# Value windows of chunked attention read back in fourteen strided transfers, with two tiles of their own and the query and key loads in between

## The chip, the core and the metric

The kernel runs on one core of one Trainium2 chip. The metric is device microseconds of that core for one execution, inputs and output in DRAM. The core has a matrix engine (PE; PEld is its weight load), a vector engine (DVE), an activation engine (ACT), GpSimd (POOL) and SyncE (SP). POOL, ACT and SP each issue DMA transfers on a queue of their own: in the profile q0 is POOL's (software_dynamic), q1 is SP's and q10 ACT's (hardware_dynamic). All three are served by the core's 16 DMA engines.

## The reference: what is computed

Chunked attention with memory rows, and behind it a layer of 8 experts of which each token uses two.

```
# attention: B=4, H=8, S=768, D=64; chunks of 32 queries
for c in range(24):
    keys, values of rows 32c-16 .. 32c+40 (cut at the ends), ahead of them 8 memory rows
    out[chunk c] = softmax(q k^T / 8) v
# x = attention output as [3072 tokens, 512]
logits = x @ w_gate + log1p(exp(x @ w_noise)) * noise     # 8 experts
top two experts of each token, softmax of their two logits as weights
out[token] = sum over the two of weight * relu(x @ w1[e]) @ w2[e]   # 512 -> 1024 -> 512
```

So each chunk needs a window of 56 rows of values (16 to the left, 32 of its own, 8 to the right) and 8 memory rows: 64 rows for each head.

## The kernel before

**Attention.** The four batch items (called batches here) are done one after the other, each in 3 steps of 256 tokens (`TP = 3`, `NT = 12` steps `i`, loop at L562). A step i makes the scores of step i+1 (`scores`, L402), turns the probabilities of step i (`turn_p`, L433), turns the attention rows of i-1 (`turn_x`, L466), multiplies with the values (`values`, L442), takes the exponentials of i+1 (`exps`, L428) and the router's logits of i-1 (`gate`, L475). Queries and keys of the next batch are turned by PE (`turn`, L387; `turns`, L546) in slots that `PLAN` (L558) names: for batch 1 all of it after `values` in step 1; for later batches half of the queries ahead of `values` in the middle step of the batch before, the rest and the keys behind it.

**Values.** `load_v(b)` (L119) loads a batch's values from DRAM into the tile `vn`, cast to bfloat16. `spread_v(b)` (L366) is two POOL copies that reorder them into `vp`. `window_v(b)` (L372) then writes the windows into `vb[b % 2]`, 128 partitions: partitions 0 to 63 hold the 64 rows of the even heads, 64 to 127 those of the odd heads, and in each partition lie 24 chunks of 4 heads x 64 values (24 pieces of 512 bytes). It is made of:

- one SP transfer that copies `vp` to a scratch tensor `vd[b % 2]` in DRAM (L374), 768 KB;
- two POOL transfers of the 8 memory rows, the same for all chunks (L378), 96 KB each;
- four POOL transfers from `vd` (L383): for even and for odd heads the first 32 rows of the windows (384 KB) and the other 24 (288 KB). Row r of chunk c is row r + 32c of `vd`, so a partition's 24 pieces are 32 KB apart in DRAM.

The spans (the transfers from `vd`) wait for the copy's landing. `values` (L453) reads all of `vb[b % 2]` with PE, first in step 3b.

**Order of the queues.** POOL's instructions are pinned in program order (`pin`, L70); PE, ACT, DVE and SP run in the order written too (L516). POOL's order for a batch is: memory rows and spans of batch b+1, queries and keys of batch b+2 (`load_kq`, L122), spread of batch b+2, values of batch b+3 (L567 to L573), all at the first step of batch b. Before the loop (L527 to L535) stand the spread and the window of batch 0, then load of values 1, queries and keys 1, spread 1, load of values 2. Since POOL works in order, a span that waits for the copy holds up all that is written behind it.

**Where the data lie.** One tile `w_all` (L64) holds the weights of all 8 experts, 16 KB in each partition for an expert (8 KB of w1, 8 KB of w2). While attention runs, its upper part is scratch (L102 to L111): the attention rows `xrow`, `vn`, the two `vb`, and `nat`, the loaded queries and keys of two batches. Experts 0, 1 and 2 are loaded during the last two batches (L574, L578); expert 2 lies under `nat` of batch 3.

**Behind attention.** The router finds, for each pair of experts, the list of tokens (`Route`, L233; lists and `decode`, L488). Attention rows are stored to `xd` in DRAM (`keep_x`, L484), and `gather_x` (L669) fetches the rows of one pair's list with an indirect POOL transfer. The gathers of the first 14 pairs are issued with the loads of experts 3 and 4 in between (L765 to L769). Then `mm1` (L705) and `mm2` (L723) do the two products of each expert for the pairs that use it, in the order of `blocks` (L746); the loads of experts 5 to 7 and more gathers are issued between them (`feed`, L857). `load_pair` (L839) fetches two experts' weights again for one list that ran over.

Of the kernel before, what the change touches and what calls it, by code (L numbers as in the profile page):

```python
# [12 lines left out]
BF16 = mybir.dt.bfloat16  # L13
# [9 lines left out]
def kernel(  # L23
# [40 lines left out]
    w_all = wpool.tile([128, E, WE], BF16, name="w_all")  # L64
    wflat = w_all.rearrange("p e c -> p (e c)")
    w1v = w_all[:, :, 0:KP * F].rearrange("p e (k f) -> p e k f", k=KP)
    w2v = w_all[:, :, KP * F:WE].rearrange("p e (f d) -> p e f d", f=FB)
# [9 lines left out]
    def load_expert(e):  # L77
        pin(nc.gpsimd.dma_start(out=w1v[:, e], in_=moe_w1[e].rearrange("(kp p) f -> p kp f", p=128)))
        pin(nc.gpsimd.dma_start(out=w2v[:, e], in_=moe_w2[e].rearrange("(fb p) d -> p fb d", p=128)))


    def load_part(e, i):
        h = slice(i % 2 * KP // 2, (i % 2 + 1) * KP // 2) if i < 2 else slice(i % 2 * FB // 2, (i % 2 + 1) * FB // 2)
        if i < 2:
            pin(nc.gpsimd.dma_start(out=w1v[:, e, h], in_=moe_w1[e].rearrange("(kp p) f -> p kp f", p=128)[:, h]))
        else:
            pin(nc.gpsimd.dma_start(out=w2v[:, e, h], in_=moe_w2[e].rearrange("(fb p) d -> p fb d", p=128)[:, h]))
# [14 lines left out]
    scol = [E * WE]  # L102
# [6 lines left out]
    vb = [scratch(2 * NCH * HP * D).rearrange("p (a c w) -> p a c w", a=2, c=NCH) for _ in range(2)][::-1]  # L109
# [261 lines left out]

    def window_v(b):  # L372
        t, o = vb[b % 2], vd[b % 2]
        nc.sync.dma_start(out=o[LC:LC + S, :].rearrange("(p s) c -> p (s c)", s=SO), in_=vp)  # L374
        for par in range(2):
            p0 = par * 64
            cols = slice(par * 256, (par + 1) * 256)
            pin(nc.gpsimd.dma_start(out=t[p0:p0 + NM, par], in_=mvn[b * NM:(b + 1) * NM, cols].unsqueeze(1).to_broadcast([NM, NCH, 256])))  # L378
        for par in range(2):
            p0 = par * 64  # L380
            cols = slice(par * 256, (par + 1) * 256)
            for r0, n in ((0, CH), (CH, WIN - CH)):
                pin(nc.gpsimd.dma_start(out=t[p0 + NM + r0:p0 + NM + r0 + n, par],  # L383
                                        in_=o[r0:r0 + S, cols].rearrange("(c k) w -> k c w", k=CH)[0:n]))
# [131 lines left out]
    with tc.manual_schedule(engines={ET.PE, ET.Activation, ET.DVE, ET.SP}):  # L516
# [10 lines left out]
        spread_v(0)  # L527
        window_v(0)
# [3 lines left out]
        load_v(1)  # L532
        load_kq(1)
        spread_v(1)
# [27 lines left out]
        for i in range(NT):  # L562
# [4 lines left out]
            if tp == 0 and more:  # L567
                window_v(b + 1)
                if b + 2 < B:
                    load_kq(b + 2)  # L570
                    spread_v(b + 2)
# [414 lines left out]
```

## Time and profile before

| | us |
|---|---|
| three runs, median (lowest, highest) | 363.06 (361.42, 363.59) |
| the profiled execution | 358.42 |
| its span (first to last instruction) | 356.7 |

| engine | busy us | share of span |
|---|---|---|
| PE | 285.9 | 80% |
| DVE | 170.3 | 48% |
| ACT | 136.9 | 38% |
| POOL | 134.3 | 38% |

| queue | packets | MB | share of 16 engines' time |
|---|---|---|---|
| q0 (POOL) | 34240 | 46.82 | 73.2% |
| q1 (SP) | 13920 | 6.62 | 10.9% |
| q10 (ACT) | 1668 | 3.02 | 2.4% |

The page cuts the span into 40 slices and gives the busy share of each in tenths. A group line gives line, engine, operation, out<-in, count, then busy time and mean ns of one, then the engine's idle time ahead of them and what ended most of it. A line of the waits reads: engine and tile waited <- for what: us in total, times, longest. A line of the timeline gives start, length, engine, line, operation, count, and in brackets the idle time ahead and what ended it. Transfers are listed with their size and the median time from issue to landing. Before, `w_all` is the name under which the trace shows `vb`, `vn`, `nat` and `xrow` too, since they are cut out of it: `w_all<-vd` are the spans, `w_all<-mvn` the memory rows, `w_all<-in_q_dram` the queries.

| stretch, us | PE busy us | POOL busy us | granted PE clock | GB/s of the DMA engines |
|---|---|---|---|---|
| 35 to 60 | 16.82 | 14.94 | 0.57 | 196 |
| 60 to 90 | 21.89 | 12.00 | 0.56 | 230 |
| 90 to 120 | 20.39 | 11.65 | 0.81 | 217 |
| 120 to 140 | 8.92 | 6.69 | 0.64 | 220 |
| 150 to 170 | 19.89 | 7.75 | 1.00 | 165 |
| 200 to 250 | 49.68 | 20.48 | 1.00 | 153 |

### The profile page before, as it was taken

The page shows a single profiled execution, that of the slowest core. Times are in us where ns is not written, and L with a number is a line of the kernel's source. Part 1 is how long each engine was busy: PE and PEld are TensorE (multiplying, and loading weights), DVE is VectorE, ACT ScalarE, POOL GpSimd, SP SyncE. Part 2 cuts the span into 40 slices and gives each one's busy share as a digit, 9 for nine tenths or more (in the row PEclk, how much of TensorE's full clock was granted, in tenths as well). Part 3 has the DMA queues.
Part 4 walks back from the last instruction along what each step waited for, and adds up shares of the span by engine and source line. Part 5 has one row for each costly group of instructions (what it writes and reads, how often), then busy time and mean ns, then how long its engine had stood idle before and what let it go on. Part 6 is the DMA issues. An engine that isn't in the chain of part 4 may idle for free.

```text
span 356.7 us, 7042 instructions
## 1 busy us (share of the span) xinstructions
PE 285.9 (80%) x2934; PEld 186.3 (52%) x2955; DVE 170.3 (48%) x349; ACT 136.9 (38%) x189; POOL 134.3 (38%) x181
## 2 busy tenths in 40 slices
PE   0356577777847732999999999999999999999991
PEld 0245455666736621865544465664455775565540
DVE  7656456699689885531133302954310334223221
ACT  8813645564645610144322343213243222243310
POOL 6460573354453036706530744332580122201122
PEclk9995655565687865699999999999999999999998
DMA  8999999999999999499999999961289971100012
GB/s 122 235 171 169 245 174 208 251 198 211 247 156 208 253 249 180 106 194 143 178 196 235 209 173 252 159 119 51 87 166 189 208 184 54 53 2 2 25 47 81
DMA packets 49866, 56.97 MB, mean 160 GB/s; under 512 B 16931, under 2 KB 39523, under 8 KB 49828
## 3 DMA queue, kind: packets, MB, share of 16 engines
q0 software_dynamic: 34240, 46.82, 73.2%
q1 hardware_dynamic: 13920, 6.62, 10.9%
q10 hardware_dynamic: 1668, 3.02, 2.4%
q8 instruction: 25, 0.41, 0.5%
q14 instruction: 13, 0.11, 0.1%
HBM read 70.39 MB, written 13.96 MB: 236 GB/s over the span
## 4 chain that ended last, share of the span: by engine, by line
PE 33%; issue 20%; POOL 5%; DVE 4%; DMA 3%; POOLq 1%; ACT 0%; DVEq 0%
PE p_h L714 18%; PE p_y L726 13%; POOL out_dram L677 4%; DMA out_dram<-y,main_dst 1%; DMA xTt<-xt 1%; DMA xt<-xd,main_src 1%; POOL xt L671 1%; DVE w_all L460 1%; PE p_xt L691 0%; POOL w_all L844 0%; POOLq L981 0%; DVE mx L423 0%; DVE sc L425 0%; ACT xT L472 0%; PE ps_o L453 0%
## 5 line engine op out<-in xcount | busy, mean ns | idle before, releaser
L714 PE MATMUL p_h<-xTt,w_all 128*128 128x256 bf16 (+3 forms) x669 | 102.7, 313 | 0.7 <-DVE xTt L692 0.5
L726 PE MATMUL p_y<-w_all,h 128*128 128x512 bf16 x446 | 102.3, 379 | 0.9
L714 PEld LDWEIGHTS <-w_all 128*128 128x128 bf16 x736 | 70.0, 101 | 36.3 <-issue 0.7
L702 ACT ACTIVATE h<-p_h 128x512 bf16<-128x512 f32 (+1 forms) x81 | 44.7, 551 | 95.9 <-PE p_h L714 88.3
L726 PEld LDWEIGHTS <-h 128*128 128x128 bf16 x464 | 45.3, 98 | 51.6
L700 DVE TENSOR_SCALAR h<-p_h 128x512 bf16<-128x512 f32 (+1 forms) x49 | 31.0, 633 | 82.8 <-PE p_h L714 73.7
L677 POOL DMA_INDIRECT out_dram<-y,main_dst x28 | 30.9, 1103 | 87.9 <-DVE y L732 75.4
L732 DVE SCALAR_TENSOR_TENSOR y<-p_y,main_w,y 128x512 f32<-128x512 f32 x28 | 21.0, 750 | 39.2 <-PE p_y L726 32.5
L393 PE MATMUL p_t<-identb,w_all 128*64 128x128 bf16 x384 | 20.6, 288 | 23.0 <-DMA w_all<-in_k_dram 13.4
L671 POOL DMA_INDIRECT xt<-xd,main_src x28 | 27.9, 997 | 24.2 <-DMA xTt<-xt 13.0
L730 ACT ACTIVATE y<-p_y,main_w 128x512 f32<-128x512 f32 x28 | 19.2, 687 | 37.0 <-PE p_y L726 36.0
L393 PEld LDWEIGHTS <-w_all 128*64 128x64 bf16 x384 | 18.1, 155 | 25.2 <-DMA w_all<-in_k_dram 13.9
L439 ACT COPY pT<-p_p 128x1024 bf16<-128x1024 bf16 x12 | 12.1, 1012 | 27.5 <-PE p_p L436 27.5
L383 POOL DMA_DIRECT2D w_all<-vd x16 | 11.8, 747 | 23.8 <-DMA vd<-vp 19.3
L460 DVE TENSOR_TENSOR w_all<-ps_o,rs 128x512 bf16<-128x512 f32 x24 | 15.6, 686 | 8.2 <-PE ps_o L453 7.8
L415 PE MATMUL ps_s<-kT,qT 128*32 128x112 bf16 x384 | 11.6, 276 | 7.2 <-DVE kT L549 5.4
L368 POOL COPY vp<-w_all 128x1536 bf16<-128x1536 bf16 x8 | 11.5, 1469 | 13.2 <-DMA w_all<-in_v_dram 13.2
L430 ACT ACTIVATE pb<-sc 128x1024 bf16<-128x1024 f32 x12 | 12.8, 1063 | 8.9 <-DVE sc L425 8.7
L549 DVE COPY kT<-p_t 64x768 bf16<-64x768 bf16 x12 | 11.5, 955 | 7.9 <-PE p_t L393 7.8
L425 DVE TENSOR_TENSOR sc<-ps_s,mx 128x1024 f32<-128x1024 f32 x12 | 14.7, 1225 | 0.8
L423 DVE TENSOR_REDUCE mx<-ps_s 128x16 f32<-128x1024 f32 x12 | 14.7, 1224 | 0.8 <-PE ps_s L415 0.5
L453 PE MATMUL ps_o<-w_all,pT 128*32 128x128 bf16 x384 | 10.9, 280 | 3.3 <-issue 2.0
(172 smaller groups left out, 284.0 us busy)
## 6 DMA issues: line engine op xcount, KB each, us to landing
w_all<-in_moe_w_dram POOLq DMA_DIRECT2D x16, 1024.0 KB, 20.7
w_all<-in_moe_w_dram POOLq DMA_DIRECT2D x8, 512.0 KB, 13.8
w_all<-in_v_dram POOLq DMA_DIRECT2D x4, 768.0 KB, 12.1
w_all<-in_k_dram POOLq DMA_DIRECT2D x4, 768.0 KB, 20.9
w_all<-in_q_dram POOLq DMA_DIRECT2D x4, 768.0 KB, 18.1
vd<-vp SPq DMA_DIRECT2D x4, 768.0 KB, 9.0
w_all<-vd POOLq DMA_DIRECT2D x8, 384.0 KB, 13.0
w_all<-vd POOLq DMA_DIRECT2D x8, 288.0 KB, 13.3
```

Source lines behind the costliest of these rows:

```text
L393: nc.tensor.transpose(out=p_t[own(par), s, :], in_=src[:, 2 * pair + par, s * D:(s + 1) * D], identity=identb, tile_position=(0, par * 64))
L423: nc.vector.tensor_reduce(out=mx, in_=s3, axis=AX, op=Alu.max)
L425: nc.vector.tensor_tensor(out=sc, in0=s3, in1=bc(mx, KW), op=Alu.subtract)
L460: nc.vector.tensor_tensor(out=xr[:, j, 0:Dm].rearrange("p (h d) -> p h d", h=H), in0=ps_o[:, j].rearrange("p c a d -> p (c a) d"), in1=bc( ...
L671: i = nc.gpsimd.indirect_dma_start(out=xts[key].bitcast(I32), out_offset=None, in_=xd, in_offset=bass.IndirectOffsetOnAxis(ap=ix, axis=0))
L677: i = nc.gpsimd.indirect_dma_start(out=out, out_offset=bass.IndirectOffsetOnAxis(ap=ix, axis=0), in_=y, in_offset=None, bounds_check=N - 1 ...
L700: nc.vector.tensor_scalar(out=out_, in0=in_, scalar1=0.0, scalar2=None, op0=Alu.max)
L702: nc.scalar.activation(out=out_, in_=in_, func=Act.Relu)
L714: nc.tensor.matmul(out=o, lhsT=w(kp * F + f * 128, 128), rhs=x[:, kp], start=(kp == 0), stop=(kp == KP - 1))
L726: nc.tensor.matmul(out=p, lhsT=h[:, (f * n + j) * 128:(f * n + j + 1) * 128], rhs=w(KP * F + f * Dm, Dm), start=(f == 0), stop=(f == FB - 1))
L730: nc.scalar.activation(out=y, in_=p, func=Act.Copy, scale=weight)
L732: nc.vector.scalar_tensor_tensor(out=y, in0=p, scalar=weight, in1=y, op0=Alu.mult, op1=Alu.add)
```

## The change

It has three parts.

- **Spans.** In place of four transfers of 32 and 24 neighbouring rows, `spans_v` issues 14, seven for the even and seven for the odd heads in turn. Transfer x takes rows x, x+7, ... x+49 of the window: eight partitions seven apart, 96 KB, 192 pieces of 512 bytes. The bytes are the same in all.
- **Homes.** The two `vb` are no longer cut from `w_all` but are tiles of their own, `w_b[0]` and `w_b[1]`, each three halves of an expert. `w_all` keeps experts 0 to 4; experts 5, 6 and 7 lie in the six halves of `w_b` (expert 6 with a half in each). The rest of the scratch moves down: `xrow` now lies over expert 4, `vn` over 3 and 4, `nat` over 2 and 3. The total size is the same.
- **Order.** The copy to `vd` is now a function `copy_v`, written behind the spread of its batch (on SP, ahead of the next load of values). POOL loads values 1 ahead of the window of batch 0. `load_kq` of the loop is gone: in `window_v(b)` the queries of batch b+1 are loaded behind the first six spans and its keys behind the other eight. So queries and keys of a batch are loaded during the window of the batch ahead of it; before, POOL issued those of batch b+2 behind the spans of b+1, which is the same place in the order but behind all spans.

```diff
--- before.py
+++ after.py
@@ -61,10 +61,16 @@
     wpool = ctx.enter_context(tc.tile_pool(name="wpool", bufs=1))
 
     WE = KP * F + FB * Dm
-    w_all = wpool.tile([128, E, WE], BF16, name="w_all")
+    WP = WE // 2
+    assert KP * F == WP and 2 * NCH * HP * D == 3 * WP
+    EA = E - 3
+    w_all = wpool.tile([128, EA, WE], BF16, name="w_all")
     wflat = w_all.rearrange("p e c -> p (e c)")
-    w1v = w_all[:, :, 0:KP * F].rearrange("p e (k f) -> p e k f", k=KP)
-    w2v = w_all[:, :, KP * F:WE].rearrange("p e (f d) -> p e f d", f=FB)
+    w_b = [wpool.tile([128, 3, WP], BF16, name=f"w_b{i}") for i in range(2)]
+    places = [(w_all[:, e, 0:WP], w_all[:, e, WP:WE]) for e in range(EA)]
+    places += [(w_b[2 * x // 3][:, 2 * x % 3], w_b[(2 * x + 1) // 3][:, (2 * x + 1) % 3]) for x in range(3)]
+    w1v = [a.rearrange("p (k f) -> p k f", k=KP) for a, _ in places]
+    w2v = [a.rearrange("p (f d) -> p f d", f=FB) for _, a in places]
 
 
     def pin(i):
@@ -75,16 +81,16 @@
             pin(i)
 
     def load_expert(e):
-        pin(nc.gpsimd.dma_start(out=w1v[:, e], in_=moe_w1[e].rearrange("(kp p) f -> p kp f", p=128)))
-        pin(nc.gpsimd.dma_start(out=w2v[:, e], in_=moe_w2[e].rearrange("(fb p) d -> p fb d", p=128)))
+        pin(nc.gpsimd.dma_start(out=w1v[e], in_=moe_w1[e].rearrange("(kp p) f -> p kp f", p=128)))
+        pin(nc.gpsimd.dma_start(out=w2v[e], in_=moe_w2[e].rearrange("(fb p) d -> p fb d", p=128)))
 
 
     def load_part(e, i):
         h = slice(i % 2 * KP // 2, (i % 2 + 1) * KP // 2) if i < 2 else slice(i % 2 * FB // 2, (i % 2 + 1) * FB // 2)
         if i < 2:
-            pin(nc.gpsimd.dma_start(out=w1v[:, e, h], in_=moe_w1[e].rearrange("(kp p) f -> p kp f", p=128)[:, h]))
+            pin(nc.gpsimd.dma_start(out=w1v[e][:, h], in_=moe_w1[e].rearrange("(kp p) f -> p kp f", p=128)[:, h]))
         else:
-            pin(nc.gpsimd.dma_start(out=w2v[:, e, h], in_=moe_w2[e].rearrange("(fb p) d -> p fb d", p=128)[:, h]))
+            pin(nc.gpsimd.dma_start(out=w2v[e][:, h], in_=moe_w2[e].rearrange("(fb p) d -> p fb d", p=128)[:, h]))
 
 
     def sidon(o, i):
@@ -99,14 +105,14 @@
     apart = "rows of one are not rows of another"
 
 
-    scol = [E * WE]
+    scol = [EA * WE]
 
     def scratch(n):
         scol[0] -= n
         return wflat[:, scol[0]:scol[0] + n]
     xrow = [scratch(SO * Dm).rearrange("p (s r) -> p s r", s=SO) for _ in range(2)]
     vn = scratch(H * SO * D).rearrange("p (h c) -> p h c", h=H)
-    vb = [scratch(2 * NCH * HP * D).rearrange("p (a c w) -> p a c w", a=2, c=NCH) for _ in range(2)][::-1]
+    vb = [t.rearrange("p x c -> p (x c)").rearrange("p (a c w) -> p a c w", a=2, c=NCH) for t in w_b]
     nat = [[scratch(H * SO * D).rearrange("p (h c) -> p h c", h=H) for _ in range(2)] for _ in range(2)]
     assert scol[0] >= 2 * WE
     mvs = w_all[0:B * NM, 0, 0:2 * H * D].bitcast(F32).rearrange("p (h d) -> p h d", h=H)
@@ -369,19 +375,34 @@
                 out=vp.rearrange("p (s a c d) -> p a c s d", s=SO, a=2, c=HP)[:, par],
                 in_=vn.rearrange("p (c a) (s d) -> p a c s d", a=2, s=SO)[:, par]))
 
+    def copy_v(b):
+        nc.sync.dma_start(out=vd[b % 2][LC:LC + S, :].rearrange("(p s) c -> p (s c)", s=SO), in_=vp)
+
+    def memory_v(b):
+        for par in range(2):
+            cols = slice(par * 256, (par + 1) * 256)
+            pin(nc.gpsimd.dma_start(out=vb[b % 2][par * 64:par * 64 + NM, par],
+                                    in_=mvn[b * NM:(b + 1) * NM, cols].unsqueeze(1).to_broadcast([NM, NCH, 256])))
+
+    XW = WIN // 8
+
+    def spans_v(b, lo, hi):
+        o = vd[b % 2]
+        for x in range(lo, hi):
+            for par in range(2):
+                p0 = par * 64 + NM + x
+                cols = slice(par * 256, (par + 1) * 256)
+                src = bass.AP(tensor=o.tensor, offset=o.offset + x * Dm + par * 256, ap=[[XW * Dm, 8], [CH * Dm, NCH], [1, 256]])
+                pin(nc.gpsimd.dma_start(out=vb[b % 2][p0:p0 + 7 * XW + 1:XW, par], in_=src))
+
     def window_v(b):
-        t, o = vb[b % 2], vd[b % 2]
-        nc.sync.dma_start(out=o[LC:LC + S, :].rearrange("(p s) c -> p (s c)", s=SO), in_=vp)
-        for par in range(2):
-            p0 = par * 64
-            cols = slice(par * 256, (par + 1) * 256)
-            pin(nc.gpsimd.dma_start(out=t[p0:p0 + NM, par], in_=mvn[b * NM:(b + 1) * NM, cols].unsqueeze(1).to_broadcast([NM, NCH, 256])))
-        for par in range(2):
-            p0 = par * 64
-            cols = slice(par * 256, (par + 1) * 256)
-            for r0, n in ((0, CH), (CH, WIN - CH)):
-                pin(nc.gpsimd.dma_start(out=t[p0 + NM + r0:p0 + NM + r0 + n, par],
-                                        in_=o[r0:r0 + S, cols].rearrange("(c k) w -> k c w", k=CH)[0:n]))
+        memory_v(b)
+        spans_v(b, 0, 3)
+        if b + 1 < B:
+            load_nat(nat[(b + 1) % 2][1], q, b + 1)
+        spans_v(b, 3, XW)
+        if b + 1 < B:
+            load_nat(nat[(b + 1) % 2][0], k, b + 1)
 
 
     def turn(b, unit):
@@ -525,13 +546,14 @@
             nc.vector.memset(vb[0][own(par), 1 - par], 0.0)
         nc.vector.tensor_copy(mvn.rearrange("m (a c d) -> m a c d", a=2, c=HP), mvs.rearrange("m (c a) d -> m a c d", a=2))
         spread_v(0)
+        copy_v(0)
+        load_v(1)
         window_v(0)
         for u in range(2 * HP):
             for o_, i_ in turn(0, u):
                 (nc.vector.tensor_copy if u % 2 else nc.scalar.copy)(o_, i_)
-        load_v(1)
-        load_kq(1)
         spread_v(1)
+        copy_v(1)
         load_v(2)
         pbs[0] = exps(scores(0))
         nc.vector.tensor_copy(wgn, wgs)
@@ -567,8 +589,8 @@
             if tp == 0 and more:
                 window_v(b + 1)
                 if b + 2 < B:
-                    load_kq(b + 2)
                     spread_v(b + 2)
+                    copy_v(b + 2)
                 if b + 3 < B:
                     load_v(b + 3)
             if i in (2 * TP, 2 * TP + 1):
@@ -840,11 +862,11 @@
         for x in range(2):
             e = nc.values_load(oi[0:1, x:x + 1], engines=[ET.Pool], min_val=0, max_val=E - 1,
                                skip_runtime_bounds_check_because="computed on chip from a table of pairs")
-            pin(nc.gpsimd.dma_start(out=w1v[:, x], in_=moe_w1[bass.ds(e, 1)].rearrange("o (kp p) f -> p (o kp) f", p=128)))
-            pin(nc.gpsimd.dma_start(out=w2v[:, x], in_=moe_w2[bass.ds(e, 1)].rearrange("o (fb p) d -> p (o fb) d", p=128)))
+            pin(nc.gpsimd.dma_start(out=w1v[x], in_=moe_w1[bass.ds(e, 1)].rearrange("o (kp p) f -> p (o kp) f", p=128)))
+            pin(nc.gpsimd.dma_start(out=w2v[x], in_=moe_w2[bass.ds(e, 1)].rearrange("o (fb p) d -> p (o fb) d", p=128)))
 
     def static_w(e):
-        return lambda c, m: w_all[:, e, c:c + m]
+        return lambda c, m: places[e][c // WP][:, c % WP:c % WP + m]
 
     steps = []
     for b, (slots, visits) in enumerate(blocks):
```

## The prediction, made before the changed kernel was run

> **What bounds the kernel now.** I read the page first: the slices for the stages, then its group lines for the spans, then the waits of PE and POOL, and last the timeline around the start of the expert stage.
>
> ```profile
> PE   0356577777847732999999999999999999999991
> DMA  8999999999999999499999999961289971100012
> L383 POOL DMA_DIRECT2D w_all<-vd x16 | 11.8, 747 | 23.8 <-DMA vd<-vp 19.3
> w_all<-vd POOLq DMA_DIRECT2D x8, 384.0 KB, 13.0
> w_all<-vd POOLq DMA_DIRECT2D x8, 288.0 KB, 13.3
> ```
>
> A slice is 8.9 us. From slice 17 (about 150 us) on PE is full: nothing on the expert stage's PE is changed, so what the change is worth is by how much earlier that stage starts. Before it DMA is full and PE is not: attention waits for transfers. The 16 span transfers are cheap to issue (11.8 us of POOL) but land 13 us later.
>
> ```profile
> PE p_t L393 <- DMA w_all<-in_k_dram: 13.4, 3, 8.5
> PE p_t L393 <- DMA w_all<-in_q_dram: 7.2, 4, 3.0
> PE ps_o L453 <- DMA w_all<-vd: 1.3, 1, 1.3
> 61.15 1.04 PE L453 MATMUL ps_o<-w_all,pT 128*32 128x128 bf16 x32 [2.03 <-issue]
> 66.19 2.96 POOL L383 DMA_DIRECT2D w_all<-vd  x4 [8.95 <-DMA vd<-vp]
> 94.23 0.80 POOL L78 DMA_DIRECT2D w_all<-in_moe_w_dram  x1 [0.83 <-DMA w_all<-in_q_dram]
> 137.47 1.61 POOL L671 DMA_INDIRECT xt<-xd,main_src  x1 [2.24 <-DVE facts L307]
> 143.04 0.59 PE L691 MATMUL p_xt<-identb,xt 128*128 128x128 bf16 x4 [3.74 <-DMA xt<-xd,main_src]
> ```
>
> The last two lines are the gate. The first gather is issued at 137.47, and PE has its rows at 143.04. In the semaphore records of the trace the last part of expert 2's weights lands at 142.64 and the first gather at 142.95: the gather stands behind six weight transfers in POOL's DMA queue. POOL issues the first of these at 94.23, but the queue gets to it only at about 105.5 (0.51 MB of weight packets are through by 108, at 0.205 MB per us), and from there to 142.6 it takes 37.1 us. So two clocks run to the gate: the DMA queue, and the compute chain, whose own gather is ready at 137.5.
>
> **The change, part by part.**
>
> *The packets of the spans.* A window is 1.376 MB, 336 packets of 4096 bytes. While spans run they take a median of 354 to 394 ns in the four windows, with 16 in flight; the first few of a window, with few in flight, and the gathers at 140 to 148 us take 159. The two transfers of memory rows (8 neighbouring partitions each) put the same 4096-byte packets at 629 ns on average when both run together. So the time goes with how many engines write into the same neighbourhood of partitions: 159 alone, about twice that for 32 rows on 16 engines, four times for eight neighbouring rows. No row has eight rows seven apart. Its bounds are 159 and 370; I take 200, nearest to the uncontended row, because neighbours no longer run together and the two halves alternate. At 370 a window costs the queue 336 x 0.37 / 16 = 7.8 us, at 200 it costs 4.2. That is 3.6 us less in each of 4 windows, 14 us of queue in all (0 to 18). This is capacity, not path: it counts only as far as POOL feeds the queue.
>
> [...]
>
> *Issue on POOL.* Four issues of 747 ns (2.96 us in the timeline) become 14. The nearest row is the transfer of memory rows, with the same 8x24x256 shape: median 670 ns (645 to 720). 14 x 0.67 = 9.4 us, 6.4 more a window, 26 us in four. The upper end is the spans' own 0.747: 10.5. SP and the other queues issue nothing more.
>
> *Waits added.* In the changed kernel's order each POOL DMA waits until the one eight before it has landed, so eight are in flight. The sixth span (and the first loads after it) wait for old loads that are home; the last span of a window waits for the query load issued eight places earlier. That load needs 3.9 us of queue (0.405 MB per 2 us) and some 2.5 us of latency against 5.4 us of issues: I take 1.2 us a window (0 to 3). Behind it stand the key load, the spread of the next values and its copy.
>
> *Order of loads.* load_v(1) goes out ahead of the spans, into the queue's hole at 20 to 22 us; the copy (7.2 us) does not wait for it. The first window's spans land about 34 instead of 32.7: it loses 1.2 us at values(0). Then query and key loads come early: of the waits of PE, values(3) (2.0), the queries of batch 2 (2.6) and 3 (0.3), and a net 2.4 at the start of batch 1 go away. The compute chain gains 2.4 + 2.0 + 2.6 + 0.3 = 7.3, so its gather is issued about 130.2; with 3.6 us to land it (issue 1.6, landing 2) that is 133.8. The key waits of batches 2 and 3 are worth nothing: DVE's routing and its key copies end last there.
>
> *Homes.* Experts 5 to 7 lie where vb was, expert 4 over the last attention rows and 3 over vn. Experts 3 and 4 are issued after gathers that need those rows in DRAM anyway, so no wait is new: 0. Cover gone, the price would be a late expert 4, which landed 17 us after its issue. PE reads the same tiles' sizes: 0.
>
> *The sum, on the profiled execution.* After the change the queue is mostly ahead, and POOL is the clock. Its cycle for a batch is 9.4 of spans, 1.8 of query and key loads, 1.2 of wait, 2.9 + 0.3 of spread: 15.6. Then SP copies the values and POOL waits L for the landing. From the first landing, 19.97: first weights issued at W = 19.97 + 3 x 15.6 + 0.8 (first window's older loads) + 3 L + 9.4 = 77 + 3 L. L in the trace is 7.2, 6.9, 11.4 and 10.2. The long two began while span packets filled the engines and a store of attention rows ran; the short two ran beside plain loads. After, a copy starts beside the key load, when the spans are through, and two of three meet such a store. I take 7.5, so W = 99.5, the queue reaches the weights 1.3 later and ends 37.1 after that: 137.9 against 142.6. That is later than the compute chain's 133.8, so it decides: 4.7 us. PE's stage moves by that. L at 6.9 gives 6.5; L as before (28.5 in three) gives -1.3. The compute chain caps the gain at 9.
>
> The profiled execution took 358.42 us (span 356.7), which is 4.6 under the median 363.06 of the three runs. The difference 4.7 is taken from the median: 358.4.
>
> **Rivals.**
>
> *The copy comes late (slower).* If L is 10.8, the mean of its two long rows, W = 109.4 and the queue ends at 147.8: 5.2 later, 368.3. The point from which it decides is L = 9.1, where W + 38.4 is 142.6. For it: the four rows average 8.9, and more traffic starts at once behind each window. Against: the long rows had span packets beside them.
>
> *Packets stay at 370 (same).* If DRAM reads of 512 bytes, not the writes, made them slow, the queue stays full as it is now and ends where it ended, less the hole of 1 to 1.5 us that load_v(1) fills: 362. For it: every span reads 512-byte pieces 32 KB apart, before and after. Against: the memory rows, read from SBUF, are slower still.
>
> *Everything overlaps (faster).* If L is near 6.5 and the last span does not wait, W = 93; the queue ends at 131.4 and the compute chain's 133.8 decides: 9 us, 354. [...]
>
> *Each transfer pays its own latency.* If transfers did not overlap, 14 at the 2.8 us of a lone gather would be 39 us a window instead of about 13: 26 x 4 = 104 more, 467. Against: the first two memory transfers landed 0.4 us apart. With eight in flight 2.8 us is 0.35 each, under the 0.67 of an issue.
>
> [...]
>
> **How the numbers follow.** Forecast case 0.50 (354 to 363, of it 0.38 beyond 1%, which is 3.6 us and about what a measurement of this kernel can tell from no change); everything overlaps 0.10; packets stay 0.17 (0.14 same, 0.03 slower); copy late 0.20 (0.04 same, 0.16 slower); own latency 0.03. Faster by over 1%: 0.38 + 0.10 = 0.48. Within: 0.12 + 0.14 + 0.04 = 0.30. Slower: 0.03 + 0.16 + 0.03 = 0.22. The range reaches from 352 (everything overlaps, and 2 us of spread between runs) to 368 (late copy); the likeliest case's own is 354 to 363.
>
> **What would show each step.** Span packets near 160 to 220 ns, not 370. 14 issues near 670 ns a window, 56 in all. POOL's wait for vd<-vp 6.5 to 8 us a window; over 9.1 and the gain is gone. The waits for queries on PE under 4 us in all. The first weight issue at 97 to 102 and the first gather's rows at PE by 135 to 140. It would be wrong if weights were issued after 104, if spans still took 350 ns, or if the expert stage, PE full today, got gaps before experts 4 to 7.

## The result, and the profile after

| | before | after |
|---|---|---|
| median of four runs each, us | 362.24 (361.29 to 363.59) | 367.7 (364.1 to 368.4) |
| ratio | | 1.014 (95% interval 1.0095 to 1.0185) |
| the profiled execution, us | 358.42 | 368.4 |
| its span, us | 356.7 | 366.8 |

The change makes the kernel 1.4 per cent slower; 1.3 per cent faster was forecast. Ratios leave out executions more than 1.5 per cent above the fastest of the same kernel, where enough others remain. First the page of the kernel after: PE and DMA in 40 slices (9.2 us each now) and the group of the span transfers.

```profile
PE   0352763666658852599999999999989999999990
DMA  8999989999959999589999999941289961100012
L396 POOL DMA_DIRECT2D w_b<-vd x56 | 34.8, 629 | 33.9 <-DMA vd<-vp 13.4
```

The issue itself came out as priced, 629 ns each and 8.7 us a window. But DMA, which before was full from slice 1 to 15, now has holes (8 in slice 5, 5 in slice 11), and PE falls to 2 in slice 3 and to 3 in slice 6, at the two longest of its waits below (6.6 us to 37.8, 7.1 us to 65.9). The waits and the timeline of the kernel after say at what:

```profile
PE ps_o L474 <- DMA w_b<-vd: 18.0, 3, 7.1
POOL w_b L396 <- DMA vd<-vp: 13.4, 3, 5.9
POOL w_b L396 <- DMA w_all<-in_q_dram: 9.8, 3, 4.3
POOL w_b L396 <- DMA w_all<-in_v_dram: 4.3, 3, 2.1
PE p_t L414 <- DMA w_all<-in_q_dram: 2.4, 1, 2.4
```

```profile
24.45 0.63 POOL L396 DMA_DIRECT2D w_b<-vd  x1 [2.11 <-DMA w_all<-in_v_dram]
25.91 0.93 POOL L123 DMA_DIRECT2D w_all<-in_q_dram  x1 [0.83 <-DMA w_b<-mvn]
26.84 4.35 POOL L396 DMA_DIRECT2D w_b<-vd  x7
33.78 0.63 POOL L396 DMA_DIRECT2D w_b<-vd  x1 [2.59 <-DMA w_all<-in_q_dram]
37.77 1.04 PE L474 MATMUL ps_o<-w_b,pT 128*32 128x128 bf16 x32 [6.62 <-DMA w_b<-vd]
88.01 0.63 POOL L396 DMA_DIRECT2D w_b<-vd  x1 [4.32 <-DMA w_all<-in_q_dram]
93.39 1.04 PE L474 MATMUL ps_o<-w_b,pT 128*32 128x128 bf16 x32 [4.34 <-DMA w_b<-vd]
109.54 0.82 POOL L84 DMA_DIRECT2D w_all<-in_moe_w_dram  x1
144.74 1.63 POOL L693 DMA_INDIRECT xt<-xd,main_src  x1 [2.23 <-DVE facts L313]
149.82 0.58 PE L713 MATMUL p_xt<-identb,xt 128*128 128x128 bf16 x4 [3.25 <-DMA xt<-xd,main_src]
```

The first window shows the pattern of the first three. POOL stops at the sixth span for a value load, at the query load for the memory rows, and at the last span for the query load; PE then waits 6.62 us for that last span. PE's waits for queries went from 7.2 us to 2.4, as the new order was to do, but its waits for values went from 1.3 to 18.0. So the first weights are issued at 109.54 (94.23 before), and PE has the first gathered rows at 149.82 (143.04 before), 6.8 us later. The last packet of the first six weight transfers is through at 149.10 (142.28 before). The span is 10.1 longer: 3.3 more come behind that point (216.98 against 213.66 from there to the end), 1.57 of it a gap on PE before 273 us that the kernel before does not have; the rest was not followed up.

### The profile page after: what moved, and what is told of

Its sections match the earlier page's. It is cut to its first block, busy times and chain, and to the rows that moved or that the text cites. A ratio compares the mean times of both kernels' runs of the same rounds, so it can differ in the third digit from the quotient of the medians.

```text
span 366.8 us, 7091 instructions
## 1 busy us (share of the span) xinstructions
PE 283.7 (77%) x2934; PEld 184.0 (50%) x2955; DVE 167.8 (46%) x349; ACT 136.3 (37%) x189; POOL 157.3 (43%) x221
## 3 DMA queue, kind: packets, MB, share of 16 engines
q1 hardware_dynamic: 13920, 6.62, 9.9%
## 4 chain that ended last, share of the span: by engine, by line
issue 25%; PE 23%; POOL 9%; DVE 4%; DMA 2%; POOLq 1%; ACT 1%; ACTq 0%; DVEq 0%
PE p_h L736 11%; PE p_y L748 9%; POOL out_dram L699 6%; POOL xt L693 2%; DMA out_dram<-y,main_dst 1%; DVE w_all L481 1%; DMA xt<-xd,main_src 1%; ACT pT L460 1%; PE ps_o L474 0%; PE p_xt L713 0%; PE p_list L358 0%; POOL w_all L866 0%; DVE h L722 0%; POOLq L1003 0%; ACT xT L493 0%
## 5 line engine op out<-in xcount | busy, mean ns | idle before, releaser
L724 ACT ACTIVATE h<-p_h 128x512 bf16<-128x512 f32 (+1 forms) x81 | 44.6, 551 | 96.3 <-PE p_h L736 80.4
L748 PEld LDWEIGHTS <-h 128*128 128x128 bf16 x464 | 45.3, 98 | 53.3 <-issue 1.9
L748 PE MATMUL p_y<-w_all,h 128*128 128x512 bf16 x285 | 65.6, 379 | 2.2 <-ACT y L752 1.6
L736 PE MATMUL p_h<-xTt,w_all 128*128 128x384 bf16 (+3 forms) x381 | 64.3, 328 | 1.4 <-issue 0.8
L736 PEld LDWEIGHTS <-w_all 128*128 128x128 bf16 x448 | 41.6, 101 | 27.1 <-issue 1.6
L396 POOL DMA_DIRECT2D w_b<-vd x56 | 34.8, 629 | 33.9 <-DMA vd<-vp 13.4
L736 PE MATMUL p_h<-xTt,w_b 128*128 128x256 bf16 (+1 forms) x288 | 38.0, 290 | 0.0
L748 PE MATMUL p_y<-w_b,h 128*128 128x512 bf16 x161 | 36.9, 379 | 0.4
L736 PEld LDWEIGHTS <-w_b 128*128 128x128 bf16 x288 | 28.1, 98 | 9.9
L414 PE MATMUL p_t<-identb,w_all 128*64 128x128 bf16 x384 | 18.4, 259 | 17.1 <-DMA w_all<-in_k_dram 8.5
L414 PEld LDWEIGHTS <-w_all 128*64 128x64 bf16 x384 | 15.6, 136 | 19.4 <-DMA w_all<-in_k_dram 8.6
L474 PE MATMUL ps_o<-w_b,pT 128*32 128x128 bf16 x384 | 10.7, 278 | 18.2 <-DMA w_b<-vd 18.0
L474 PEld LDWEIGHTS <-pT 128*32 128x32 bf16 x384 | 8.1, 124 | 18.5 <-issue 18.4
L451 ACT ACTIVATE pb<-sc 128x1024 bf16<-128x1024 f32 x12 | 12.8, 1063 | 9.2 <-DVE sc L446 9.2
```

The lines of the kernel that those rows point to most:

```text
L396: pin(nc.gpsimd.dma_start(out=vb[b % 2][p0:p0 + 7 * XW + 1:XW, par], in_=src))
L414: nc.tensor.transpose(out=p_t[own(par), s, :], in_=src[:, 2 * pair + par, s * D:(s + 1) * D], identity=identb, tile_position=(0, par * 64))
L474: nc.tensor.matmul(out=ps_o[r * CH:(r + 1) * CH, j, pair], lhsT=pT[:, j * HP + pair, r * CH:(r + 1) * CH], rhs=vb[b % 2][:, :, (tp * 2 + j ...
L724: nc.scalar.activation(out=out_, in_=in_, func=Act.Relu)
L736: nc.tensor.matmul(out=o, lhsT=w(kp * F + f * 128, 128), rhs=x[:, kp], start=(kp == 0), stop=(kp == KP - 1))
L748: nc.tensor.matmul(out=p, lhsT=h[:, (f * n + j) * 128:(f * n + j + 1) * 128], rhs=w(KP * F + f * Dm, Dm), start=(f == 0), stop=(f == FB - 1))
```

## The experiments

The change is taken apart first, then one size in it is changed, then the suspected cost is put in alone. Ratios are to the kernel before on the same chip (medians of 362.6, 359.8, 359.9 and 360.1 us in the four groups of runs).

### The change in its parts

**The homes alone**: four spans a window, loads in the old order, the two window tiles as in the change.

```diff
+    w_b = [wpool.tile([128, 3, WP], BF16, name=f"w_b{i}") for i in range(2)]
```

> Only the homes are changed; the spans are four transfers and the loads stand in the old order. Theory 1 (eight DMAs in flight: the last span of a window waits for the query load) and theory 2 (the number of issues on POOL) both expect the time before, 362 within 2 us, and the first weights issued at about 94. A rival, that the new homes cost time in the expert stage, expects 364 to 367 with the start of the expert stage unmoved at 143.

Measured: 363.95 us, ratio 1.0025 (0.9982 to 1.0067). The homes cost nothing that can be measured.

**Homes and fourteen spans**, the loads still in the old order: values, queries and keys behind the window.

```diff
     def window_v(b):
         memory_v(b)
-        spans_v(b, 0, 3)
-        ...
+        spans_v(b, 0, XW)
```

> The homes and the fourteen spans, the loads in the old order: values 1, queries and keys behind all spans. Theory 1 (the wait for the query load is what costs) expects no long wait on POOL between spans, packets near 280 ns, and 358 to 362. Theory 2 (fourteen issues of 0.63 us make POOL the clock, whatever the order) expects the first weights at 104 or later and 365 to 369.

Measured: 368.65 us, 1.0157 (1.0108 to 1.0206). There is no load between the spans here, and the loss is the whole of the change's. So the wait at the query load, which the result seems to blame, is not needed for it. POOL does wait at the spans, 7.0 us for value loads and 3.6 for key loads, and the first weights are issued at 111.21.

**Homes and order**, with four spans of neighbouring rows, the queries between the even and the odd heads' spans.

```diff
+        spans_v(b, 0, 1)
+        load_nat(nat[(b + 1) % 2][1], q, b + 1)
+        spans_v(b, 1, 2)
+        load_nat(nat[(b + 1) % 2][0], k, b + 1)
```

> The homes and the new order, but with four spans: the query load stands between the spans of the even and of the odd heads. Theory 1 and theory 2 expect about the time before, 360 to 364, since with few transfers nothing waits for the load eight places before and POOL issues little. Theory 3 (the query load between the spans makes the values late for PE) expects 364 to 368 with PE waiting over 8 us for spans.

Measured: 368.98 us over eight runs, which scatter widely (364.69 to 373.38); the ratio is 1.0122 (1.0077 to 1.0166). Order by itself costs about 1 per cent too, with PE waiting 17.1 us for values (in the slowest of the eight, which was the one profiled). The two losses do not add up: both together are 1.014.

**The change with its query load behind all fourteen spans.**

```diff
-        spans_v(b, 0, 3)
+        spans_v(b, 0, XW)
         if b + 1 < B:
             load_nat(nat[(b + 1) % 2][1], q, b + 1)
-        spans_v(b, 3, XW)
```

> The changed kernel with one thing undone: the query load stands behind all fourteen spans, just ahead of the key load. Theory 1 expects POOL's wait for the query load to go (9.8 us in three windows), the first weights 8 to 12 us earlier than 109.5, and 359 to 363. Theory 2 expects only 1 to 2 us of the 5.5, so 365 to 367. Theory 3 (PE waits because half the spans land behind the query load) expects PE's wait for spans to fall from 18 us to under 8.

Measured: 365.45 us, 1.0091 (1.0059 to 1.0123). PE's waits for values fall from 18.0 to 3.0 us, and those for queries rise from 2.4 to 12.0. The late data changed its name. The loss is 0.9 per cent in place of 1.4, but the two intervals overlap. The first weights are issued at 109.31 (109.54 in the change): without the wait for the query load POOL waits 8.9 us at the spans for value loads and 14.9 for the copy. So the theory that this wait is what costs, which expected the weights 8 to 12 us earlier, falls.

### Another number of rows in a span

All three keep the old order of loads. Only how the 56 rows are dealt out differs: 28 rows two partitions apart (four spans a window, as many as before), 14 rows four apart (eight spans), 4 rows fourteen apart (28 spans). A fourth run leaves the fourteen spans as they are and lets SP issue them.

```diff
-    XW = WIN // 8
+    XW = WIN // 14
...
-                src = bass.AP(tensor=o.tensor, offset=o.offset + x * Dm + par * 256, ap=[[XW * Dm, 8], [CH * Dm, NCH], [1, 256]])
+                src = bass.AP(tensor=o.tensor, offset=o.offset + x * Dm + par * 256, ap=[[XW * Dm, 14], [CH * Dm, NCH], [1, 256]])
```

> The homes, the loads in the old order, and four spans a window as before, but each of 28 rows two partitions apart in place of 32 or 24 rows side by side. The number of issues is that of the kernel before (4 x 0.74 us a window). Theory of the issues: the number of spans sets the time, so 362 to 365, the 363.95 of four spans side by side, less whatever the packets gain. If spreading the rows is worth something by itself, packets of 4096 bytes are shorter than the 366 to 423 ns of the spans before and the time is 359 to 362. Rival (rows apart cost the DMA engines more than rows side by side): 366 to 369.

> The homes, the loads in the old order, and eight spans a window of 14 rows four partitions apart. Theory of the issues: ten spans more a window cost 4.7 us in the whole (368.65 against 363.95), so four more cost 1.9: 365 to 367. Rival (what costs is that the rows are apart, not how many issues there are): 367 to 370, as with fourteen.

> The homes, the loads in the old order, and 28 spans a window of four rows fourteen partitions apart: twice the transfers of the change, the same bytes. Theory of the issues: 14 more a window at 0.47 us of time each (the slope between four and fourteen) give 375; if nothing is left to hide them, 14 x 0.63 x 4 windows are 35 us and the time nears 400; so 373 to 400. Rival (what costs is the rows being apart, which they are as well with fourteen spans): 367 to 370.

Measured: 28 rows 352.65 us, 0.9821 (0.9779 to 0.9864); 14 rows 352.14, 0.9795 (0.9747 to 0.9842); 4 rows 399.3, 1.1096 (1.1042 to 1.115). Both few-span kernels beat the kernel before by 2 per cent, more than any theory expected. The straight line from four to fourteen spans that the expectation for eight drew was wrong, since its four-span end had neighbouring rows. With rows apart it costs nothing to go from four spans to eight. From eight to fourteen it costs 3.6 per cent, 13 us, where POOL's spans take 14.8 us more to issue (34.8 against 20.0); from fourteen to 28 it costs 9.4 per cent, 34 us, for 37.5 us more (72.3).

```diff
-                pin(nc.gpsimd.dma_start(out=vb[b % 2][p0:p0 + 7 * XW + 1:XW, par], in_=src))
+                nc.sync.dma_start(out=vb[b % 2][p0:p0 + 7 * XW + 1:XW, par], in_=src)
```

> The kernel with the homes, the loads in the old order and fourteen spans a window, all of its spans issued by SP in place of POOL. The kernel with POOL issuing them took 368.65 us, the one with four spans 363.95. Theory of the issues (each span costs POOL 0.63 us in order, and in a window POOL has 5.7 us more to issue than before): POOL has nothing to issue, so its next load is asked for at once, and the time is that of four spans or a little less, 359 to 364. Rival (the fourteen transfers themselves, or their packets, cost the DMA engines more, whoever issues them): 367 to 370. What would speak for neither: SP issues more slowly than POOL, which the issue rows of SP will show.

Measured: 419.02 us, 1.1641 (1.1586 to 1.1697): neither theory's number. The timeline of SP, its waits and the times of its issues (shortest, median and longest, in ns) say why.

```profile
19.45 27.40 SPq L396 DMA_DIRECT2D w_b<-vd  x14
61.31 31.76 SPq L396 DMA_DIRECT2D w_b<-vd  x14
100.04 37.86 SPq L396 DMA_DIRECT2D w_b<-vd  x14
SPq L396 <- DMA xd<-w_all: 58.9, 3, 28.1
L396 SPq DMA_DIRECT2D w_b<-vd x56: 654/655/5118, 19.5 to 175.9; - x56
```

Half of SP's issues take 0.655 us and less, about what POOL's take (0.63), though some take up to 5.1. But behind the eleventh or twelfth span of the last three windows SP stands until a store of attention rows (`xd<-w_all`, issued by ACT) has landed, 58.9 us in all, and PE waits 45.3 us for values. So this run does not tell POOL's time from the transfers; two runs below do.

### The order again, with eight spans

The change's own order, with spans of 14 rows (four ahead of the query load, four behind); the same with queries and keys behind all spans; and with both ahead of the spans, this once with 14 rows and once with the change's eight.

```diff
-        spans_v(b, 0, 3)
+        spans_v(b, 0, 2)
         ...
-        spans_v(b, 3, XW)
+        spans_v(b, 2, XW)
```

> The change in everything but the size of its spans: eight of 14 rows four partitions apart in place of fourteen of eight rows seven apart, four ahead of the load of the queries and four behind it. It issues 5.0 us of spans a window on POOL in place of 8.7 (the 625 ns each that the same spans took in the old order). Theory of the issues with the end of the values (a window's spans hold up POOL's cycle by their issue, and PE by when the last of them lands): the cycle of a window is 3.7 us shorter than the change's, and 3 to 4 windows give 11 to 15 us: a ratio to the kernel before of 0.975 to 0.985 if the load between the spans is harmless, as it was with fourteen spans (1.014 with it, 1.016 without). Rival (the load of the queries between the spans makes values late by itself): the last four spans land some 6 to 7 us later, as they did in the change, and the ratio is 0.99 to 1.005.

> As the run with the change's order and spans of 14 rows, but the queries are loaded behind all spans, with the keys; the copies and the value loads keep the change's place. Theory: the values land as early as in the old order (10 us from the first issue to the last landing), and the next copy goes out ahead of the next window: ratio 0.97 to 0.98, the 0.9795 of the old order or a little less. Rival (queries and keys come too late for PE): 0.985 to 0.995, with waits of PE on the queries and keys of over 3 us each window.

> As the run with the change's order and spans of 14 rows, but queries and keys are loaded ahead of a window's spans, while POOL waits for the copy. Theory: POOL has 1.8 us less to issue behind the wait, and the loads fill the queue while it waits; but the spans then stand behind 1.5 MB of loads, 7 to 9 us at the 170 to 217 GB/s of these stretches, so the values come late for PE: ratio 0.985 to 1.01. Rival (the loads are over by the time the copy has landed, 6 to 8 us later): 0.965 to 0.98, a new best.

> The change with its fourteen spans a window, but queries and keys loaded ahead of the spans, while POOL waits for the copy. Theory of the issues: fourteen issues a window still stand in POOL's cycle, so no order of the loads brings the time below that of before: ratio 1.005 to 1.02 (the two other orders gave 1.009 and 1.016). Rival (it is the order that costs: loads between or behind the spans): with nothing between and nothing behind, the packets' gain comes through, 0.975 to 0.995.

Measured: the change's order 353.69 us, 0.985 (0.9808 to 0.9892); queries behind 350.98, 0.9762 (0.9734 to 0.9789), the best of all; queries first 357.37, 0.9951 (0.9915 to 0.9987); queries first with fourteen spans 367.46, 1.0215 (1.0169 to 1.0261). So the change with eight spans in place of fourteen, and nothing else touched, would have been 1.5 per cent faster. Against queries behind the spans, a query load between them costs 0.9 per cent and queries and keys ahead of them 1.9, with PE waiting 7.3 and 11.8 us for values in place of 1.6. The waits of the change with eight spans, and then the page of the best kernel:

```profile
PE ps_o L474 <- DMA w_b<-vd: 7.3, 1, 7.3
POOL w_b L396 <- DMA w_all<-in_v_dram: 7.2, 3, 3.3
PE p_t L414 <- DMA w_all<-in_q_dram: 2.4, 1, 2.4
```

```profile
PE   0355676688576616999999999999999999999990
DMA  8999999999999995898999999930599931100011
L396 POOL DMA_DIRECT2D w_b<-vd x32 | 20.1, 633 | 32.4 <-DMA vd<-vp 22.0
```

Of the three waits of the change for values one is left, in the first window, and in the best kernel none over 1.6 us. There DMA is full up to slice 14 again, PE does not fall under 5 between slices 2 and 13, and POOL waits for the copy (22.0 us in all) and at the spans for value loads (8.8), but for no query load.

One step more, the best order with spans of 28 rows, brought nothing:

> The best so far (copies ahead, queries and keys behind all spans, eight spans of 14 rows: 0.976) with four spans of 28 rows, two partitions apart, in their place: 2 us less of issue on POOL a window, but packets of 316 to 342 ns in the median in place of 287 to 312. With four and eight spans alike in the old order (0.982 and 0.980): 0.97 to 0.985. Rival (rows two apart do worse beside the value load that runs with them here): 0.985 to 1.

Measured: 352.35 us, 0.9794 (0.9747 to 0.984).

### POOL's time by itself

Into the kernel with eight spans in the old order, eight copies on POOL that nothing uses are put in each window: one behind each span, or all behind the last.

```diff
+    def spin_pool():
+        pin(nc.gpsimd.tensor_copy(out=spin, in_=spin))
...
                 pin(nc.gpsimd.dma_start(out=vb[b % 2][p0:p0 + 13 * XW + 1:XW, par], in_=src))
+                spin_pool()
```

> The kernel with eight spans of 14 rows in the old order (0.9795 of the time before), and behind each span a copy of 352 columns on POOL that nothing uses: by the 1.48 us of a copy of 1536 columns some 0.35 to 0.5 us, so 2.8 to 4 us a window, about what six more spans of 0.62 cost. Transfers and packets stay those of eight spans. Theory (POOL's time is what the six further spans cost): the ratio goes to that of fourteen spans, 1.005 to 1.02. Rival (it is the number of transfers, what each holds up in the queue): 0.975 to 0.99.

> The same eight copies on POOL, but all behind the last span of the window, so that the spans land as early as without them and only POOL's cycle is longer. If what costs is POOL's cycle (the next loads, the spread and the next window come later), the ratio is that of the copies between the spans, 1.005 to 1.02. If what costs is that the last span lands later, it is 0.975 to 0.99.

Measured: behind the last span 365.97 us, 1.0157 (1.0108 to 1.0206), the ratio of fourteen spans; behind each span 359.11, 1.0005 (0.9967 to 1.0043), between the two theories. The eight copies take 3.9 us of POOL, where six more spans take 3.7. The waits of the kernel with the copies behind the spans, and then those of the kernel with fourteen spans in the old order:

```profile
POOL vp L374 <- DMA w_all<-in_v_dram: 8.0, 2, 5.3
PE p_t L417 <- DMA w_all<-in_q_dram: 15.2, 4, 7.9
PE p_t L417 <- DMA w_all<-in_k_dram: 13.0, 3, 8.3
```

```profile
POOL vp L374 <- DMA w_all<-in_v_dram: 8.2, 2, 5.2
PE p_t L409 <- DMA w_all<-in_q_dram: 15.7, 4, 7.9
PE p_t L409 <- DMA w_all<-in_k_dram: 12.5, 3, 8.7
```

They are alike to half a microsecond; only a wait of 2.1 us for values stands in the second alone. The longest single wait, for the queries of batch 2, ends at 70.91 us in the one and at 70.87 in the other. POOL work that issues nothing does all that six more transfers do: loss by POOL's time is shown, loss by the number of transfers is not needed. It acts through POOL's cycle, for the spans of the kernel with copies land as early as without (8.2 and 9.5 us from first issue to last packet in the first two windows, 9.0 and 11.4 without). Between the spans the copies cost less because they fill time in which POOL waited: from its first span to its first weight issue POOL waits 23.8 us with them, 32.2 without copies and 30.7 with the copies behind. So of 15.8 us of copies 5.4 remain in its cycle (82.1 against 76.7), and behind the spans 14.0.

**Fourteen spans of neighbouring rows**, as many issues as in the change, old order.

```diff
-                p0 = par * 64 + NM + x
+                p0 = par * 64 + NM + r
...
-                src = bass.AP(tensor=o.tensor, offset=o.offset + x * Dm + par * 256, ap=[[XW * Dm, 8], [CH * Dm, NCH], [1, 256]])
+                src = bass.AP(tensor=o.tensor, offset=o.offset + r * Dm + par * 256, ap=[[Dm, 8], [CH * Dm, NCH], [1, 256]])
```

> Fourteen spans a window of eight rows side by side in place of eight rows seven partitions apart, in the old order; the number of issues is the same, so POOL is as busy as in the kernel with fourteen spans apart (1.016). Theory (with fourteen spans POOL's issue sets the time, and the packets are off the path): packets of 366 ns and more as in the kernel before, and yet a ratio of 1.01 to 1.03. Rival (rows apart are worth with fourteen spans what they are worth with four, 0.02): 1.03 to 1.045.

Measured: 376.88 us, of six runs two at 370.49 and 373.32 and four at 376.86 to 380.12; ratio 1.0446 (1.0383 to 1.0509), and 1.033 by the two alone. Either lies in the rival's range and not in the theory's, the second only just. The packets are longer still than before (medians of 434 to 548 ns); the same number of spans with rows seven apart, 1.0157, is 2.9 per cent better, or 1.7 by the two. Rows apart are worth something with fourteen spans too; POOL's issue took more than that back.

### All of it in one table

"To weights" is the time from POOL's first span to its first weight issue. The waits are PE's totals in the profile, for values (`ps_o`), queries and keys (`p_t`); of the keys the first wait, 8.3 to 8.9 us in every kernel, is left out. The last column is the issue of the first gather. The run with SP is not in it, since POOL issues no span there.

| kernel | spans | ratio | to weights, us | values + queries + keys, us | sum | gather at |
|---|---|---|---|---|---|---|
| queries behind, 14 rows | 8 | 0.976 | 74.2 | 1.6 + 4.0 + 3.9 | 9.5 | 129.96 |
| queries behind, 28 rows | 4 | 0.979 | 70.6 | 2.0 + 4.9 + 3.1 | 10.0 | 134.42 |
| old order, 14 rows | 8 | 0.980 | 76.7 | 0 + 4.9 + 5.3 | 10.2 | 133.05 |
| old order, 28 rows | 4 | 0.982 | 70.0 | 0 + 6.6 + 5.4 | 12.0 | 133.58 |
| change's order, 14 rows | 8 | 0.985 | 73.4 | 7.3 + 2.4 + 0 | 9.7 | 135.24 |
| queries first, 14 rows | 8 | 0.995 | 79.2 | 11.8 + 2.4 + 0 | 14.2 | 138.56 |
| 14 rows, POOL copies between | 8 | 1.001 | 82.1 | 0 + 5.6 + 7.2 | 12.8 | 138.21 |
| before | 4 | 1 | 74.3 | 1.3 + 7.2 + 4.9 | 13.4 | 137.47 |
| homes alone | 4 | 1.003 | 76.1 | 2.7 + 6.6 + 3.0 | 12.3 | 141.52 |
| queries behind, 8 rows | 14 | 1.009 | 89.7 | 3.0 + 12.0 + 5.1 | 20.1 | 143.50 |
| change's order, neighbouring rows | 4 | 1.012 | 81.9 | 17.1 + 2.4 + 0 | 19.5 | 149.69 |
| the change | 14 | 1.014 | 90.3 | 18.0 + 2.4 + 0 | 20.4 | 144.74 |
| old order, 8 rows | 14 | 1.016 | 91.5 | 2.1 + 15.7 + 3.8 | 21.6 | 146.49 |
| 14 rows, POOL copies behind | 8 | 1.016 | 90.7 | 0 + 15.2 + 4.7 | 19.9 | 145.84 |
| queries first, 8 rows | 14 | 1.022 | 92.3 | 21.9 + 2.4 + 0 | 24.3 | 147.19 |
| 8 neighbouring rows | 14 | 1.045 | 95.8 | 16.3 + 6.8 + 5.8 | 28.9 | 147.61 |
| old order, 4 rows | 28 | 1.110 | 127.0 | 29.4 + 9.6 + 7.0 | 46.0 | 178.03 |

Two things are to be read in it. Where POOL needs about 90 us and more, PE waits about 20 us and more, in every order of the loads; with fourteen spans the order mostly decides whether they are called values or queries. And the gather moves with these waits. The order with neighbouring rows is an exception that no run explains: there PE waits 19.5 us with POOL at 81.9. (A wait ahead of values which the profile calls "issue" is not in the sum: 5.6 us in the row of the homes, 3.6 in that of 4 rows, 2.5 in that of queries behind with 28 rows, 2.0 in that of before and up to 2.1 elsewhere.)

When an issue costs nothing, and when it costs its whole time, is shown by the four kernels with rows apart in the old order. POOL's busy time and its waits are those from its first span to its first weight issue; the last packet is that of the first six weight transfers.

| spans | POOL busy, us | POOL waits, us | first weight issue at | last weight packet at | between, us |
|---|---|---|---|---|---|
| 4 | 35.7 | 34.3 | 89.48 | 136.78 | 47.3 |
| 8 | 44.6 | 32.2 | 96.49 | 136.23 | 39.7 |
| 14 | 58.4 | 33.1 | 111.21 | 150.81 | 39.6 |
| 28 | 96.0 | 31.0 | 146.59 | 185.66 | 39.1 |

POOL's waits hardly shrink when its issues grow. With four spans the weights stand some 8 us longer in the DMA queue than with more: POOL is that far ahead of it. Eight spans use this lead up and cost nothing; from there on the last packet is later by what the issue is later (14.6 and 14.7 us from eight spans to fourteen). The copies behind the spans do the same: weights issued at 110.89, the last packet at 149.81.

## Why the prediction was wrong, by its own steps

*The packets*, taken at 200 ns, averaged 339, 294 and 315 ns in the change's first three windows, and 214 in the fourth, where no load stands between the spans (medians 295, 278, 277 and 173). The direction was right, and the gain is real: 2 per cent with four spans (1.0025 to 0.982). The medians of a window's 4096-byte packets (memory rows counted in) are 434 to 548 ns for eight neighbouring rows, 355 to 386 for 32 and 24 neighbours before the change, 316 to 342 for 28 rows two apart, 287 to 312 for 14 four apart, 172 to 274 for eight seven apart and 178 to 207 for four fourteen apart; all but those of before are from the old order with the new homes. They are in line with the prediction's reading, that the time goes with how many engines write into the same neighbourhood of partitions, but that was the author's inference: no run changes the number of engines alone, and none shows what makes neighbours slow. Of eight rows seven apart, only two windows had a median of 180 or less, near the 159 of the uncontended row: the change's fourth (179) and the first of the old order with fourteen spans (172).

*Issue on POOL*, 9.4 us a window: measured 8.7. Right, and yet the cost that sank the change. The prediction did put 6.4 us more into POOL's cycle (5.7 measured). But it counted on the cycle's waits to shrink by nearly as much: from its first span to its first weight issue POOL waited 38.7 us before, for W = 99.5 it could have waited only about 22 (an estimate: 99.5 less 19.97, less the 57.7 that POOL was busy in the change), and it waited 32.6.

*Waits added*, 1.2 us a window, is the step that failed. Measured were 5.5, 4.3 and 5.6 us in the three windows. The prediction held that the sixth span and the loads behind it wait "for old loads that are home": they waited 2.11 us for the value load and 0.83 for the memory rows, both issued eight places earlier. (That POOL waits for the transfer eight places earlier shows in the kernel before too: its query load at 72.11 waited 2.96 us for a key load, and the key load at 76.45 waited 3.42 for a value load.) And it gave the query load an empty queue: the last span waited 2.59, 2.84 and 4.32 for it. That is 11 us more than 3 x 1.2 + 0.8 for the three windows. What the runs showed in its place is more than a size: with the query load behind the spans this wait is gone, POOL waits as long in its cycle for value loads and the copy (32.0 us in place of 32.6), and the weights are issued at 109.31.

*Order.* The compute chain was to gain 7.3 us, with values(0) 1.2 us late. The waits for queries did fall by 4.8. But the spans of the first three windows took 17.5, 18.0 and 19.4 us from first issue to last packet (11.7, 14.2 and 19.7 before), and PE stood 18.0 us for values. The chain's gather came at 144.74, not 130.2. The prediction asked only whether the last span waits; it did not follow PE behind it.

*L*, 7.5: measured 8.75, 8.37 and 8.4, so 3.0 us more in three. *Homes*, 0: right.

*The sum*: W was to be 99.5 and is 109.54. Waits 11, L 3.0, issue 3 x 0.7 less for the three cycles and 0.7 for the last spans, and a landing 0.7 earlier: 10.5, against 10.0. From there on the prediction held: W + 38.4 is 147.9, and the last weight packet is through at 149.10. The rival "copy late" gave 368.3, nearly the time measured, with another mechanism: L stayed under its break-even of 9.1.

Against the theories of the runs: that the query load between the spans is the cause fell with the old order at 1.016. It is a second cost, 0.9 per cent with eight spans against the queries behind them; the 0.5 with fourteen is not clear of the noise. Why 28 rows and 14 rows stand so close, with POOL's cycle 6.7 us apart, is seen in POOL's lead over the queue (the table above): their last weight packets are through at 136.78 and 136.23. The copies between the spans issue the weights 5.3 us later than without, their last packet is 4.5 later, and the profiled execution 4.7 longer (357.02 against 352.28); the ratios are 2.1 per cent apart (1.0005 against 0.9795), 7.5 us, and where the rest goes is open. Open too is why the change's order costs so much with neighbouring rows.

## What to carry to other kernels

A transfer cut into more pieces was paid for here on the queue that issues them (0.63 us of POOL for each span), in order, with all the loads behind it; price the cut by that engine's cycle, free only as long as the engine is ahead of its DMA queue (here some 8 us with four spans, nothing with eight), and find the smallest number of pieces that still spreads the rows. When PE waits for data in turn, moving one load ahead of another can just change the name of the wait (here 1.3 us for values and 7.2 for queries became 18.0 and 2.4): sum the waits for all operands before and after, and ask whether the issuing engine's cycle has become shorter. A wait on a transfer some places earlier in the queue has to be priced from a full queue (forecast 1.2 us a window, measured 2.59 to 4.32 at the last span alone).

## What the runs showed of the hardware

- POOL's issue hardly depended on the size of the transfer: 757 ns for 28 rows of 24 pieces, 633 for 14, 629 for eight, 654 for four.
- SP issued half of the same transfers of eight rows of 24 pieces in 0.655 us and less, and some in up to 5.1; POOL takes 0.63 on average. SP's queue moved them in packets of 512 bytes, POOL's in packets of 4096: with the spans on SP its queue had 25120 packets and 12.13 MB, in the change 13920 and 6.62; a window of 1.376 MB on POOL is 336 packets.
- An arrangement of rows was worth 2 per cent of this kernel: 28 rows two partitions apart in place of 32 and 24 side by side, with the same four issues a window (1.0025 to 0.982).
